# Dense and dilated attention on one core: closer local tiles, contiguous raised copies and three more blocks a period on VectorE

## The chip, the core and the metric

The kernel runs on one core of a Trainium2 chip. The metric is the device time of one execution in microseconds (us), the median of several runs. The kernel before has a median of 811.33 us over 3 runs (809.96 to 811.34). A core has a matrix engine (TensorE, PE in the profile), a vector engine (VectorE, DVE), an engine for exponentials and the like (ScalarE, ACT), a general one (GpSimd, POOL) and one that issues transfers (SyncE, SP).

## What is computed

Two attentions over the same input of 2048 positions and 512 columns, both with 32 heads of 16 columns, are mixed by a gate for each position. The first ("A") attends to all positions. The second ("B", the local one) attends to 8 positions, two apart, up to the own one. All tensors are bfloat16.

```python
def reference(A_x, A_wqkv, A_wo, B_x, B_wqkv, B_wo, gate_w):
    ...
        scores = jnp.einsum("bhqd,bhkd->bhqk", q, k) * (Dh ** -0.5)
        p = _softmax(scores, axis=-1)
        o = jnp.einsum("bhqk,bhkd->bhqd", p, v)
    ...
        W, dil = 8, 2
    ...
        logits = jnp.einsum("bhsd,bhswd->bhsw", q, kg) * scale
        logits = jnp.where(mask[None, None, :, :], logits, -1e9)
        attn = _softmax(logits, axis=-1)
        o = jnp.einsum("bhsw,bhswd->bhsd", attn, vg)
    ...
    g = _sigmoid((x * gate_w).sum(-1, keepdims=True))
    return g * a + (1 - g) * b
```

## The kernel before

**Dense attention.** The work is cut into 32 *periods*: 4 chunks of 512 queries by 8 groups of 4 heads. A period has 64 *blocks*, one for each of 16 key tiles (128 keys) and 4 heads. A block is a score matmul (128 keys by 512 queries, into PSUM), an exponential, and a matmul with the values into the period's accumulator. Blocks reach ACT in *sets*, by turns of 3 and 2 (`set_sizes`), in two PSUM areas (`ring`); one ACT instruction takes a set and writes `pT` in bfloat16.

**Blocks on VectorE.** Some blocks of each period are not given to ACT. `n_dve` says how many: from 3 in the first periods to 12 in all from the seventh on. These are always blocks of the last key tiles (`dve_tiles`, 4 tiles by 4 heads, so 16 at most), in groups of 3 (`NGR`). `d_set` makes them. The score matmul writes a PSUM bank. A *first pass* (`p1`) on DVE scales the scores and writes them as 16-bit integers whose bits, read as bfloat16, approximate the exponential; they go to a buffer of 3 x 512, `dt_a` or a part of `wkv` (whose weights are no longer needed by then). When a group of 3 is full, three *raises* (`sh`, m = 1 to 3) add a constant 32 m to the integers and write the sum into one of three buffers in `pd_a`. PE multiplies the group and each raised copy by values weighted for that copy (`vd_all`), four products for each block, and their sum mends most of the approximation's error. A buffer of `pd_a` has 3 rows of 514 elements (`ROW`), of which 512 are used; the raise reads its input as 6 runs of 256 and writes 3 runs of 512 with a gap of 2 between rows.

At the end of a period DVE transposes the accumulator (`accT`), POOL (DVE in the last two periods) scales it into `ott`, and every second period DVE transposes that into `oat`.

**Local attention.** `b_tile(t)` makes 16 tiles of 128 positions. PE projects keys, values and queries, DVE evicts them (`kvs`, `kvs`, `qb`), SyncE stores keys and values to DRAM and loads them back shifted for the window, in halves (`ksh`, `vsh`; three buffers). POOL does products and sums (`prod`), subtracts the maximum (`lg<-lg,mx`), ACT takes the exponential (`lg<-lg`), DVE sums (`ssum`, `rr`), POOL normalises, weighs the values and adds (`av`, part of it by accumulating transfers that POOL issues), ending in `obb`; PE transposes that and DVE copies it to `obt`. When a chunk's dense and local parts are there, PE multiplies both by the output weights, DVE evicts, SyncE stores.

**What sets the order.** Every piece of work is an `Op` with engine, estimated cost (`occ` or `parts`), due time and dependencies. `list_schedule` plans all engines against each other: an operation that can start, with the earliest due time, goes next. The code is emitted in the planned order, and each engine keeps it: an engine that waits for an instruction holds up all that stand behind it. A pair `(True, x)` in `parts` is planned on a port that DVE and POOL are taken to share, `(False, x)` is not. Due times of the dense part come from `S0`, a running count of blocks on ACT. Those of local tile t come from `BT[t]`, which begins at `b_start` and grows by `b_space`; the release is 70 us ahead of it. PE also gets matmuls of zeros (`z`) in gaps, planned so that it stays active.

Nearly all instructions are issued through two helpers: line 367 for DVE, ACT, POOL and SyncE, line 376 for matmuls (line 1200 and 633 for transposes on PE). So the profile's groups are told apart by tile names.

Of the kernel before, what the change touches and what calls it, by code (L numbers as in the profile page):

```python
# [16 lines left out]

CFG = dict(
    set_sizes=(3, 2),
    n_dve=(3, 3, 6, 6, 9, 9, 12, 12) + (12,) * 24,  # L20
    dve_tiles=4,
    b_start=36.0,
    b_space=(44.0,) * 4 + (47.0,) * 4 + (49.0,) * 8,
    chain=("pe", "dve", "act", "pool", "sp"),
)

# [4 lines left out]
DIL = 2  # L31
QW = 512
NEG = -1.0e9
BITS = 128.0
LN2 = 0.6931471805599453
SHIFT = 175.0
# [2 lines left out]
NGR = 3  # L39
# [3 lines left out]
ROW = QW + 2  # L43
# [3 lines left out]
NPD = 3  # L47
# [7 lines left out]
def _ap(base, dims):  # L55
    return bass.AP(tensor=base.tensor, offset=base.offset, ap=[list(d) for d in dims])
# [51 lines left out]
PVU, PVN = 100.0, 4  # L108
GP = lambda kind, n: [(False, PRE), (True, NS[kind] * n)]
SB = lambda n: [(True, 0.065 + n / 3840.0)]  # L110
TT = lambda n: [(True, 0.075 + n / 960.0)]
PASS, SWITCH, KEEP, RIDE, ALONE = 0.22, 0.1, 1.2, 50.0, 3.0
WAIT, FREE, LATE, CLAMP = 0.15, 0.1, 10.0, -1.0
# [3 lines left out]
SH_LAT = 0.3  # L117
# [187 lines left out]
def kernel(  # L305
# [69 lines left out]
    def mm(out, lhsT, rhs, start, stop, **kw):  # L375
        return chain(nc.tensor.matmul(out, lhsT=lhsT, rhs=rhs, start=start, stop=stop, **kw))  # L376
# [16 lines left out]
    def op(eng, occ, fn, dl, **kw):  # L393
        if any(tk.kind == "misc" for tk in kw.get("use", ())):
            dl -= URG[eng]
        o = Op(eng, occ, fn, dl, **kw)
        ops.append(o)
        return o
# [17 lines left out]
    n_dve = cfg["n_dve"]  # L416
# [3 lines left out]
    for pi in range(NP):  # L420
        first_unit.append(nu)
        n = n_dve[pi]
# [14 lines left out]
    for pi, (own, groups) in enumerate(seq):  # L437
        n = sum(len(g) for g in groups)
# [54 lines left out]
    pd_a = const.tile([128, (NPD + NPG) * NGR * ROW], BF16, name="pd_a")  # L493
# [181 lines left out]
    def k_bound(i, dl):  # L675
# [15 lines left out]
        def fill(s0, s1):  # L691
            def s():
                V.tensor_scalar(out=kt_all[:, i, s0:s1], in0=kt_all[:, i, s0:s1], scalar1=rowc[:, 1:2],
                                scalar2=negk[:, i:i + 1], op0=ALU.mult, op1=ALU.add)
            return s
# [3 lines left out]
        if i == 0:  # L699
            o_k[i] = [op("dve", 0.0, fill(sc * QW, (sc + 1) * QW), dl + 0.1 * sc, deps=[c], parts=SB(QW)) for sc in range(NC)]  # L700
        else:
            o_k[i] = [op("dve", 0.0, fill(0, S), dl, deps=[c], parts=SB(S))] * NC

    o_k = {}

    def k_pair(i, dl, rel):
# [48 lines left out]
        for e in range(2):  # L755
            o_k[i + e] = [op("dve", 0.0, fill(e), dl + 3.0 + 20.0 * e, deps=[m], parts=SB(S))] * NC

# [14 lines left out]
    def v_proj(h0, h1, tb, TB, tag, dl, rel=0.0):  # L772
# [34 lines left out]
        if nt > 0:  # L807
            d = op("dve", 0.0, evd, dl + 2.0, deps=[c], parts=TT((NV - 1) * nt * (h1 - h0) * (DH + 1)))
            for t in range(t0, tb + TB):
# [14 lines left out]
    def q_proj(pi, tag, dl, rel=0.0):  # L824
# [24 lines left out]
        c = op("dve", 0.61, ev, dl - 0.5, deps=[b], use=[tk, tq])  # L849
        o_q[pi] = op("dve", 0.0, ab, dl, deps=[c], use=[tq], parts=SB(QW))  # L850

# [3 lines left out]
    def q_pair(pi, dl, rel):  # L855
# [42 lines left out]
        c = op("dve", 0.61, ev, dl - 7.0, deps=[a], alloc=[tqs], use=[tk])  # L898
        b = op("dve", 0.0, ab, dl - 6.8, deps=[c], alloc=[tqa], use=[tqs], parts=SB(QW))
        np_ = 0.5 if i < NK1 else 1.0  # L900
# [54 lines left out]
    def b_tile(t):  # L955
# [75 lines left out]
        def logits_out(hf, wp):  # L1031
            def s():
# [5 lines left out]
                if hf == 1 and wp + WP == WH and t * 128 < DIL * (W - 1):  # L1038
                    G.affine_select(out=lg[:], in_=lg[:], compare_op=ALU.is_ge, fill=NEG,
                                    base=t * 128, pattern=[[0, H], [-DIL, W]], channel_multiplier=1)  # L1040
# [115 lines left out]
        for g_ in range(len(halves)):  # L1156
# [5 lines left out]
        a = op("dve", 0.34, sm_pre, tb + SMD, deps=[l1], use=[tlg])  # L1162
        a = op("dve", 0.0, sm_sub, tb + SMD, deps=[a], use=[tlg], parts=TT(H * W)) if SM_V else op(
            "pool", 0.0, sm_sub, GFIRST, deps=[a], use=[tlg], parts=GP("ff", H * W))
# [4 lines left out]
        if SM_V:  # L1169
            a = op("dve", 0.1, sm_gate, tb + SMD, deps=[a, o_g])  # L1170
            a = op("dve", 0.0, sm_mul, tb + SMD, deps=[a], use=[tlg], parts=TT(H * W))
        else:
# [117 lines left out]
    d_st, d_last, d_sh = {}, [None, None], []  # L1290
    d_count, d_ends, d_sg = [0, 0, 0, 0], [], []

    def d_set(pi, gi, t, j, qk_, tn):

        c_, i = periods[pi]
        late = pi >= LATE0
        key = (pi, gi)
        first = key not in d_st
        if first:
            slot = d_count[0] % NDL if late else d_count[2] % NDE  # L1300
            d_count[0] += late
            d_count[2] += not late
            d_st[key] = dict(dt=dt_bufs[slot], td=tok("dtl", NDL) if late else tok("dt", NDE), js=[], ts=[], p1=[])
        g = d_st[key]
        n_ = len(g["js"])
        g["js"].append(j)
        g["ts"].append(t)

        st = {}
        tx = tok("misc", 2)  # L1310

        def dq():
            st["x"] = misc_ps([128, QW])
            mm(st["x"][:], kt_all[32 * j:32 * j + 32, i, t * 128:(t + 1) * 128], qt_tiles[pi][32 * j:32 * j + 32, :],
               True, True, tile_position=(32 * j, 0))

        def p1():
            V.tensor_scalar(out=g["dt"][:, n_ * QW:(n_ + 1) * QW].bitcast(U16), in0=st["x"][:], scalar1=float(DH) ** -0.5 * BITS / LN2,
                            scalar2=(127.0 + DEXP + SHIFT * float(DH) ** -0.5 / LN2) * BITS, op0=ALU.mult, op1=ALU.add)
        deps = [o_q[pi], o_k[i][t // TPC], o_vd[(4 * i + j, t)]]  # L1320
        if first and late and d_count[0] <= NDL:
            deps += wkv_users + d_ends[-NV * NDE:]
        a = op("pe", 0.0, dq, tn - 3.0, mode="r", js=[j], deps=deps, alloc=[tx] + ([g["td"]] if first else []),
               use=[q_tok[pi]] + ([] if first else [g["td"]]), after=[qk_, d_last[1]], ride=True, name=f"dq{pi}")
        d_last[1] = a
        o = op("dve", 0.61, p1, tn + P1D, deps=[a], use=[tx, g["td"]], after=[d_last[0]], name=f"p1_{pi}")
        d_last[0] = o
        g["p1"].append(o)
        if len(g["js"]) < NGR:
            return  # L1330
        vs = [o_vd[(4 * i + j_, t_)] for t_, j_ in zip(g["ts"], g["js"])]

        def on_pool(m):
            return m == NV - 1 and gi in POOL_G

        def sh(m, pb):
            def s():
                o_, i_ = pb.bitcast(U16)[:, :, 0:QW], g["dt"].bitcast(U16)
                i_ = _ap(i_, [list(i_.ap[0]), [QW // 2, 2 * NGR], [1, QW // 2]])
                (G if on_pool(m) else V).tensor_scalar(out=o_, in0=i_, scalar1=STEP * m, scalar2=None, op0=ALU.add)  # L1340
            return s

        def pv(m, pb):
            def s():
                for n1, (t_, j_) in enumerate(zip(g["ts"], g["js"])):
                    pv_mm(pi, t_, j_, pb[:, n1, 0:QW], vd_all[:, m - 1, t_ - (NT - NTD)] if m else vp_all[:, t_])
            return s

        def dpv(m, pb, deps, use, dl):
            b = op("pe", 0.0, pv(m, pb), dl, mode="c", js=g["js"], full=1, deps=deps + [o_t0[pi]] + vs,  # L1350
                   use=[use, acc_tok[pi]], name=f"dpv{pi}")
            o_pv[pi].append(b)
            d_ends.append(b)
        dpv(0, g["dt"].rearrange("p (q n) -> p q n", q=NGR), list(g["p1"]), g["td"], tn + 4.5)
        for m in range(1, NV):
            if on_pool(m):
                pb = pd_bufs[NPD + d_count[3] % NPG]
                d_count[3] += 1
                tp = tok("pg", NPG)
                a = op("pool", 0.0, sh(m, pb), GFIRST, deps=list(g["p1"]), alloc=[tp], use=[g["td"]], name=f"sg{pi}",  # L1360
                       after=d_sg[-1:], parts=GP("one", NGR * QW))
                d_sg.append(a)
            else:
                pb = pd_bufs[d_count[1] % NPD]
                d_count[1] += 1
                tp = tok("pd", NPD)
                a = op("dve", 0.0, sh(m, pb), tn + 1.5 + SHD * (m - 1), deps=list(g["p1"]), alloc=[tp], use=[g["td"]],
                       lat=0.065 + NGR * QW / 1920.0 + SH_LAT, after=d_sh[-1:],
                       parts=[(False, 0.065 + NGR * QW / 1920.0)], name=f"sh{pi}")
                d_sh.append(a)  # L1370
            dpv(m, pb, [a], tp, tn + 4.5 + SHD * m)

    pend, dwait = [], []
    for k, us in enumerate(sets):
        ring = "rA" if k % 2 == 0 else "rB"
        n = len(us)
# [34 lines left out]
    for pi, (c_, i) in enumerate(periods):  # L1411
# [37 lines left out]
        if by_v:  # L1449
            a = op("dve", 0.0, po2a, E + 4.0, deps=[a, o_gr], use=[tr_], parts=TT(BPC))  # L1450
            a = op("dve", 0.0, po2b, E + 4.0, deps=[a], alloc=al, use=us, parts=TT(BPC * DH))
        else:
# [139 lines left out]
```

## Time and profile before

| | |
|---|---|
| median of 3 runs | 811.33 us |
| the profiled execution | 811.55 us |
| its span, first to last instruction | 809.7 us |
| granted TensorE clock, mean | 0.995 |
| blocks on ACT (340 sets of 3, 340 of 2) | 1700 |
| blocks on DVE (`p1`), raises | 348, 348 |
| start of the last local tile's exponential on ACT | 743.98 us |

A page of the profile gives busy time and share of the span for each engine, then the chain of work that ended last, followed back from the last instruction. The groups have one line for each kind of instruction: line, engine, operation, output <- inputs (partitions x elements and type), count, then busy time in all and mean in ns of one, then the engine's idle time before them and what ended it. Timelines have the start, the time from the first start to the last end of equal instructions that follow each other, the instruction, its count, and in brackets the idle time before it with what released it. Busy shares in the table of windows are us in that stretch, followed by the granted clock of PE, the share of the transfer engines, and GB/s. An instruction's duration holds a little overlap with the next of its engine, so the distance between starts is what a further one costs.

### The profile page before, as it was taken

The numbers are of one execution on the slowest core, as the hardware profiler recorded it, in microseconds if no ns is written. First come the engines' busy times: TensorE is split into PE (matmuls) and PEld (weight loads), VectorE is DVE, ScalarE is ACT, GpSimd is POOL, SyncE is SP. The second block draws the span as 40 slices with busy tenths as digits, with TensorE's granted clock in tenths as the row PEclk, the third lists the DMA queues.
The fourth block names the chain that finished last, engine by engine and source line by source line (L and its number), as shares of the span: only waits on it lengthen the run. The fifth ranks groups of instructions, "written<-read, shape, count | busy, mean of one in ns | idle before, by whom it ended". The sixth has DMA issues, their size and how long they took to land.

```text
span 809.7 us, 17412 instructions
## 1 busy us (share of the span) xinstructions
PE 744.5 (92%) x6637; PEld 241.5 (30%) x6694; DVE 695.4 (86%) x1080; ACT 782.8 (97%) x704; POOL 633.0 (78%) x1067
## 2 busy tenths in 40 slices
PE   8999999999989999989999999998988999889897
PEld 4333333332322222222222222222222222222232
DVE  5638786989886999999988899898998999898896
ACT  3999999999999999999999999999999999999996
POOL 4097979999979699599999469899989419899910
PEclk9999999999999999999999999999999999999999
DMA  7503071635244432526352433616271422522000
GB/s 262 138 13 111 25 173 42 147 101 143 81 96 106 92 96 73 147 85 138 98 121 62 93 99 111 136 53 139 66 176 33 105 90 67 132 60 73 1 1 27
DMA packets 58883, 77.17 MB, mean 95 GB/s; under 512 B 3744, under 2 KB 50848, under 8 KB 58800
## 3 DMA queue, kind: packets, MB, share of 16 engines
q1 hardware_dynamic: 52608, 53.91, 21.4%
q0 software_dynamic: 6048, 22.02, 14.4%
q8 instruction: 52, 0.85, 0.4%
q14 instruction: 31, 0.25, 0.1%
q10 hardware_dynamic: 144, 0.13, 0.0%
HBM read 43.78 MB, written 10.26 MB: 67 GB/s over the span
## 4 chain that ended last, share of the span: by engine, by line
ACT 49%; PE 27%; issue 20%; DVE 2%; DMA 1%; SPq 0%; ACTq 0%
ACT pT L367 49%; PE misc_ps L376 18%; PE ring L376 8%; DMA xld<-in_A_x_dram 1%; DVE pd_a L367 1%; ACT lg L367 1%; DVE accT L367 0%; PE pxt L633 0%; DVE kt_all L367 0%; DVE wkv L367 0%; DVE dt_a L367 0%; ACT xT L367 0%; SPq L367 0%; DVE qa L367 0%; DVE oat L367 0%
## 5 line engine op out<-in xcount | busy, mean ns | idle before, releaser
L367 ACT ACTIVATE pT<-ring 128x1536 bf16<-128x1536 f32 (+1 forms) x680 | 775.0, 1331 | 10.9 <-PE ring L376 7.3
L376 PE MATMUL ring<-qt,kt_all 32*128 32x512 bf16 x1700 | 268.7, 383 | 48.0 <-ACT pT L367 40.4
L367 POOL TENSOR_TENSOR prod<-ksh,qb 128x256 f32<-128x256 bf16 x256 | 171.5, 726 | 46.0 <-DMA ksh<-kv_scr 35.5
L376 PE MATMUL misc_ps<-pT,vp_all 128*17 128x512 bf16 (+1 forms) x1700 | 207.0, 385 | 0.1
L376 PEld LDWEIGHTS <-kt_all 32*128 32x128 bf16 x2048 | 90.6, 91 | 301.9 <-issue 294.0
L367 DVE TENSOR_SCALAR pd_a<-wkv 128x1536 uint16<-128x1536 uint16 x192 | 175.4, 941 | 0.6
L367 POOL TENSOR_TENSOR prod<-prod 128x256 f32<-128x256 f32 (+1 forms) x256 | 169.7, 679 | 5.2
L367 DVE TENSOR_SCALAR wkv<-misc_ps 128x512 uint16<-128x512 f32 x192 | 129.2, 682 | 24.2 <-PE misc_ps L376 21.8
L367 DVE TENSOR_SCALAR pd_a<-dt_a 128x1536 uint16<-128x1536 uint16 x156 | 142.6, 941 | 3.5 <-PE misc_ps L376 2.7
L376 PE MATMUL misc_ps<-z 128*32 128x512 bf16 x412 | 136.7, 390 | 1.6 <-DVE z L367 1.6
L376 PE MATMUL misc_ps<-pd_a,vd_all 128*17 128x512 bf16 x1044 | 135.1, 382 | 0.6 <-DVE pd_a L367 0.5
L376 PE MATMUL misc_ps<-qt,kt_all 32*128 32x512 bf16 x348 | 128.7, 382 | 4.3 <-DVE accT L367 2.1
L367 DVE TENSOR_SCALAR dt_a<-misc_ps 128x512 uint16<-128x512 f32 x156 | 104.5, 683 | 23.8 <-PE misc_ps L376 21.7
L367 POOL TENSOR_TENSOR prod<-vsh,lg 128x256 f32<-128x256 bf16 x128 | 82.2, 746 | 0.0
L376 PEld LDWEIGHTS <-vp_all 128*17 128x17 bf16 (+1 forms) x2048 | 53.5, 88 | 83.3 <-issue 71.6
L367 POOL TENSOR_TENSOR av<-vsh,lg 128x256 f32<-128x256 bf16 x128 | 77.6, 642 | 0.0
L376 PE MATMUL misc_ps<-bw,xT 128*128 128x512 bf16 x160 | 50.1, 384 | 1.7 <-issue 1.1
L376 PEld LDWEIGHTS <-vd_all 128*17 128x17 bf16 x1044 | 35.4, 88 | 54.3 <-issue 45.7
L376 PEld LDWEIGHTS <-z 128*32 128x32 bf16 x412 | 36.2, 96 | 46.5 <-issue 24.6
L376 PEld LDWEIGHTS <-xT 128*128 128x128 bf16 x576 | 29.1, 97 | 33.3 <-issue 29.5
L376 PE MATMUL misc_ps<-wkv,vp_all 128*17 128x512 bf16 x192 | 31.5, 384 | 0.0
L367 DVE CAST kvs<-misc_ps 128x512 bf16<-128x512 f32 x32 | 21.9, 684 | 10.8 <-PE misc_ps L376 10.8
(97 smaller groups left out, 519.6 us busy)
## 6 DMA issues: line engine op xcount, KB each, us to landing
ksh<-kv_scr SPq DMA_DIRECT2D x32, 512.0 KB
vsh<-kv_scr SPq DMA_DIRECT2D x32, 512.0 KB
av<-prod POOLq DMA_DIRECT2D x28, 512.0 KB, 5.6
av<-av POOLq DMA_DIRECT2D x14, 512.0 KB, 4.6
kv_scr<-kvs SPq DMA_DIRECT2D x16, 256.0 KB
qt<-q_scr SPq DMA_DIRECT2D x30, 128.0 KB
out_dram<-osb SPq DMA_DIRECT2D x15, 128.0 KB
xld<-in_A_x_dram SPq DMA_DIRECT2D x3, 512.0 KB
```

What stands on the lines that cost most here:

```text
L367: return chain_on(key, f(*a, **k))
L376: return chain(nc.tensor.matmul(out, lhsT=lhsT, rhs=rhs, start=start, stop=stop, **kw))
```

## The change

Three things are changed. The distances of local tiles become 43 us for all 16, where they were 44 (four), 47 (four) and 49 (eight). The last three periods (29, 30 and 31, from `FLAT0` on) give 15 blocks instead of 12 to DVE. In these three periods a raise reads 1536 elements in one run and writes 1536 in one run, without the gap between rows, into the same buffers; the planner costs it at 0.1 + 1536 / 3840 us on the shared port, where the others have 0.065 + 1536 / 1920 us off it.

```diff
-    n_dve=(3, 3, 6, 6, 9, 9, 12, 12) + (12,) * 24,
+    n_dve=(3, 3, 6, 6, 9, 9, 12, 12) + (12,) * 21 + (15,) * 3,
...
-    b_space=(44.0,) * 4 + (47.0,) * 4 + (49.0,) * 8,
+    b_space=(43.0,) * 16,
...
+FLAT0 = 29
...
+PT = lambda n: [(True, 0.1 + n / 3840.0)]
...
                 o_, i_ = pb.bitcast(U16)[:, :, 0:QW], g["dt"].bitcast(U16)
-                i_ = _ap(i_, [list(i_.ap[0]), [QW // 2, 2 * NGR], [1, QW // 2]])
+                if pi < FLAT0:
+                    i_ = _ap(i_, [list(i_.ap[0]), [QW // 2, 2 * NGR], [1, QW // 2]])
+                else:
+                    o_ = o_.rearrange("p q n -> p (q n)")
...
                 pb = pd_bufs[d_count[1] % NPD]
+                if pi >= FLAT0:
+                    k0 = d_count[1] % NPD * NGR * ROW
+                    pb = pd_a[:, k0:k0 + NGR * QW].rearrange("p (q n) -> p q n", q=NGR)
...
-                       lat=0.065 + NGR * QW / 1920.0 + SH_LAT, after=d_sh[-1:],
-                       parts=[(False, 0.065 + NGR * QW / 1920.0)], name=f"sh{pi}")
+                       lat=(0.065 + NGR * QW / 1920.0 if pi < FLAT0 else 0.1 + NGR * QW / 3840.0) + SH_LAT, after=d_sh[-1:],
+                       parts=[(False, 0.065 + NGR * QW / 1920.0)] if pi < FLAT0 else PT(NGR * QW), name=f"sh{pi}")
```

## The prediction

> **What bounds the kernel now.** I read the page first: its head, the busy shares and the chain that ended last.
>
> ```profile
> span 809.7 us, 17412 instructions
> PE 744.5 (92%) x6637; PEld 241.5 (30%) x6694; DVE 695.4 (86%) x1080; ACT 782.8 (97%) x704; POOL 633.0 (78%) x1067
> ...
> ACT 49%; PE 27%; issue 20%; DVE 2%; DMA 1%; SPq 0%; ACTq 0%
> ```
>
> ScalarE (ACT) is busy for 97% of the span. Only an engine that makes ACT wait can cost time, and only work taken from ACT can win any. So the next views are what ACT does, grouped by shape, and what it waits for.
>
> ```profile
> L367 ACT ACTIVATE pT<-ring 128x1536 bf16<-128x1536 f32 x340 | 524.0, 1541 | 9.8 <-PE ring L376 6.3 <-PE misc_ps L376 2.9
> L367 ACT ACTIVATE pT<-ring 128x1024 bf16<-128x1024 f32 x340 | 380.8, 1120 | 1.2 <-PE ring L376 1.0
> ...
> ACT pT L367 <- PE ring L376: 7.3, 9, 4.4
> ACT osb L367 <- PE misc_ps L376: 3.8, 1, 3.8
> ACT pT L367 <- PE misc_ps L376: 2.9, 3, 1.5
> ```
>
> The 680 exponentials hold 340 x 3 + 340 x 2 = 1700 blocks of 512 columns. Of the 7.3 us, 4.4 us is the one wait ahead of the first exponential; so between first and last they stall for 7.3 - 4.4 + 2.9 = 5.8 us in all. Their price is read from ACT's timeline, where instructions overlap a little and the distance of starts counts.
>
> ```profile
> 743.98 0.49 ACT L367 ACTIVATE lg<-lg 128x256 f32<-128x256 f32 x1
> 744.28 27.30 ACT L367 ACTIVATE pT<-ring 128x1536 bf16<-128x1536 f32 x24
> 771.81 29.79 ACT L367 ACTIVATE pT<-ring 128x1536 bf16<-128x1536 f32 x26 [0.23 <-PE ring L376]
> 805.41 1.07 ACT L367 CAST osb<-misc_ps 128x512 bf16<-128x512 f32 x2 [3.81 <-PE misc_ps L376]
> ```
>
> Twenty-four sets, by turns of 3 and 2, are 60 blocks in 27.30 us: **0.455 us a block**, gapless. The last one ends at 771.81 + 29.79 = 801.60; from there to 809.7 runs a tail of 8.1 us. Around the span lie 811.55 - 809.7 = 1.85 us in this execution (811.55 against a median of 811.33).
>
> **Part one: nine blocks leave ACT.** Three periods give 15 instead of 12 blocks to VectorE (DVE): ACT has 9 fewer exponentials, 9 x 0.455 = **4.1 us**. The built program agrees: 1691 blocks in 677 sets. On PE a moved block has a score and four products (one per weighted copy) where it had a score and one: 9 x 3 = 27 matmuls more, beside 412 on zeros that fill time which PE has to spare, so no cost there. The gain is real only if DVE keeps up in these periods. PE's filling, and DVE near the end:
>
> ```profile
> L376 PE MATMUL misc_ps<-z 128*32 128x512 bf16 x412 | 136.7, 390 | 1.6 <-DVE z L367 1.6
> ...
> 778.91 0.70 DVE L367 STREAM_TRANSPOSE accT<-misc_ps 128x512 f32<-128x512 f32 x1
> 785.60 1.28 DVE L367 TENSOR_SCALAR wkv<-misc_ps 128x512 uint16<-128x512 f32 x2
> 793.02 5.24 DVE L367 TENSOR_SCALAR pd_a<-wkv 128x1536 uint16<-128x1536 uint16 x6
> 802.08 0.72 DVE L367 STREAM_TRANSPOSE accT<-misc_ps 128x512 f32<-128x512 f32 x1 [3.82 <-PE misc_ps L376]
> ```
>
> A first pass out of PSUM costs 1.28 - 0.68 = 0.60 us of pitch, a raise (5.24 - 0.94) / 5 = 0.86 us. Twelve of each are 17.5 us, in a period of 52 x 0.455 = 23.7 us; the last raise ends 3.8 us ahead of the last transpose.
>
> **Part two: raises written contiguously.** No row shows such a raise. The nearest rows are these:
>
> ```profile
> L367 DVE TENSOR_SCALAR pd_a<-wkv x192: 892/943/955, 243.2 to 797.3; 128x1536 uint16<-128x1536 uint16 x192
> L367 DVE TENSOR_SCALAR kt_all<-kt_all,rowc,negk x11: 406/812/1219, 17.6 to 177.7; 128x2048 bf16<-128x2048 bf16 x7, 128x512 bf16<-128x512 bf16 x4
> L367 DVE TENSOR_SCALAR qa<-qs x15: 278/586/2496, 22.8 to 727.5; 128x256 uint32<-128x256 uint32 x15
> 37.11 0.81 DVE L367 TENSOR_SCALAR kt_all<-kt_all,rowc,negk 128x2048 bf16<-128x2048 bf16 x1
> ```
>
> The second is contiguous in and out: 0.81 us for 2048 columns against 0.41 for 512, 0.26 ns a column. Scaled to 1536 that is 0.41 + 1024 x 0.26 = 0.68 us, with two pointer scalars that a raise lacks. The other bound: if today's 0.94 us is a fixed 0.14 and a rate that doubles, 0.14 + 0.40 = 0.54 us. I take **0.57**, nearer the lower end (both scalars of a raise are constants), so a pitch of 0.49. At the far ends stand 0.94 (nothing gained) and 0.54. Then 15 x 0.60 + 15 x 0.49 = 16.4 us in a period of 49 x 0.455 = 22.3 us: DVE is freer than before, and its saving is off the path. The cover is this slack of some 4 us after the transposes and gate work (1.5 us); without the faster raise it would be 15 x (0.60 + 0.86) + 1.5 = 23.4 us, more than the period.
>
> The rows also say what speaks against this form. Today's raise takes 892 to 955 ns whether GpSimd (POOL) works or, as at 793, does not. The masking of qa, contiguous too, takes 278 ns at best, 586 at the median and 2496 at worst. [...]
>
> **Part three: local tiles follow closer.** Nothing is added: 16 tiles, planned 43 us apart instead of 44, 47 and 49. Where they stand now, and POOL's gaps:
>
> ```profile
> 364.70 0.63 POOL L367 TENSOR_TENSOR lg<-lg,mx 128x256 f32<-128x256 f32 x1
> 404.10 0.63 POOL L367 TENSOR_TENSOR lg<-lg,mx 128x256 f32<-128x256 f32 x1
> 412.82 0.50 ACT L367 ACTIVATE lg<-lg 128x256 f32<-128x256 f32 x1
> 443.88 0.63 POOL L367 TENSOR_TENSOR lg<-lg,mx 128x256 f32<-128x256 f32 x1 [0.18 <-DVE mx L367]
> 452.63 0.52 ACT L367 ACTIVATE lg<-lg 128x256 f32<-128x256 f32 x1
> 473.13 2.56 POOL L367 TENSOR_TENSOR prod<-ksh,qb 128x256 f32<-128x256 bf16 x4 [9.13 <-DVE qs L367]
> 662.94 0.22 POOL L367 TENSOR_TENSOR rden<-rden,g_rw 128x16 f32<-128x16 f32 x1 [15.02 <-DVE rden L367]
> 770.39 1.43 POOL L367 TENSOR_TENSOR obb<-av 128x256 bf16<-128x256 f32 x2
> ```
>
> Where tiles already follow closely POOL turns one out in 39.4 to 39.8 us; elsewhere it idles, 9 and 15 us at a time. In the built order of ACT, the local softmax's exponentials stood after block 120, 198 ... 1488, 1575; now after 120, 193 ... 1363, 1455: 90 blocks a tile between second and last, 90 x 0.455 + 0.3 = 41.3 us. POOL fits with 1.5 us to spare, and its result is ready 8.1 us before ACT asks (404.10 + 0.63 to 412.82). So I charge ACT **nothing**; cover is this 8 us lead, and gone it would cost ACT whatever POOL overruns. The last tile's exponential moves 120 blocks, 54.6 us, forward to 689; POOL's last sum, which ends 27.8 us after it now (771.8 - 744.0), ends at about 717. Period 29 starts at block 1544, about 730: contiguous raises meet POOL only in the scaling of attention outputs of two periods. SyncE's queue gets the same transfers, ksh and vsh nearer to each other and moved past q_scr and out_dram stores; a late qt is what could hurt, and has the lead of two periods.
>
> DVE's work on a tile is packed closer too. Its rows, and those for what this can do:
>
> ```profile
> L367 DVE CAST kvs<-misc_ps 128x512 bf16<-128x512 f32 x32 | 21.9, 684 | 10.8 <-PE misc_ps L376 10.8
> L367 DVE COPY obt<-misc_ps 128x512 bf16<-128x512 bf16 x16 | 6.6, 410 | 0.0
> ...
> 300.00:350.00 50.00, 46.76 (x404) 13.72 (x407) 49.28 (x74) 50.00 (x46) 39.33 (x68) 1.00 0.36 93
> 235.00:245.00 10.00, 9.74 (x70) 2.52 (x73) 7.92 (x14) 8.78 (x9) 7.65 (x14) 0.87 0.69 167
> 565.00:575.00 10.00, 9.77 (x73) 2.81 (x72) 8.60 (x14) 8.77 (x8) 9.69 (x18) 0.83 0.10 28
> 233.92 0.37 PE L376 MATMUL misc_ps<-qt,kt_all 32*128 32x512 bf16 x1 [1.88 <-DVE accT L367]
> 234.25 0.61 PE L376 MATMUL misc_ps<-z 128*32 128x512 bf16 x1
> ```
>
> Three evictions of 0.68 and four short operations of about 0.4 us each (copy, two reductions, a reciprocal) are 3.6 us a tile, in 41.3 instead of some 47 us: 0.25 us more in a period of 23.7 us until 717, then none. At 300 to 350 DVE is busy for 49.3 of 50 us and ACT never waits. But twice, at a period's turn, PE stood still (1.88 us for a transpose on DVE), its granted clock fell to 0.87 and 0.83 in those stretches, matmuls took 0.61 us, and ACT lost 10 - 8.78 = 1.2 us in each. These are accidents of the order, and the order is new from block 120 on. I take their number as unchanged, bounds from none (5.8 us of stalls gone) to four more (4 x 1.2 = 4.9 us).
>
> **The sum.** 811.55 - 4.1 - 0 - 0 = 807.4; against the median 811.33, 807.2. I say **807.3 us**.
>
> **Rivals.**
> First, *more stalls at turns of periods* (slower): DVE is denser until 717, a transpose or raise comes late, PE stands still behind it in order (with the next scores queued behind), the clock falls. For: the row at 233.92. Against: 300 to 350 above. From 3.4 more such accidents on (4.1 / 1.2) the gain is gone; with six more, 807.3 + 7.2 = 814.5. The place is between 200 and 717.
> Second, *POOL falls behind* (slower): at over 41.3 us a tile the lead of 8 us melts, over 14 tiles from 41.9 us each on (8 / 14); at 42.5 ACT waits 14 x 1.2 - 8 = 9 us, 816. For: waits of POOL on its own accumulating transfers. Against: 39.4 us when close.
> Third, *the contiguous raise is no faster*, by its form or by a busy POOL: 23.4 us of DVE against 22.3 of ACT, 1.1 us a period, 3.3 in all; 810.6, no change.
> Fourth, *stalls vanish too*, because DVE and PE are relieved in the last 90 us and the turns fall otherwise: up to 3 us of the 5.8; 804.3.
>
> **How the numbers follow.** Forecast 0.64 (its own range 805.6 to 809.0), fourth 0.13, third 0.08, first 0.11, second 0.04. A difference under 0.2%, 1.6 us, can't be told from none here. Faster than 809.7: the forecast, the fourth, and a little of the third, 0.78; same 0.10, from the third and a mild first; slower 0.12. The range takes in the fourth at 804.3 and the third at 810.6 and leaves out the two slower ones, 0.15, and some 0.05 below: 804.0 to 810.8.
>
> **What would show it.** ACT: 677 exponentials, busy about 4 us less, stalls between first and last of 4 to 8 us. Raises of 128x1536 in two groups, the 45 contiguous ones near 0.57 us and none over 1.5; last raise some 5 us ahead of the last transpose. POOL's last sum near 717, POOL at nought after about 760. POOL's lead before each ACT lg still 6 us or more. Wrong would be: ACT waits named "POOL lg", clock below 0.9 in more than two stretches of 10 us, or raises near 0.94 us.

## The result and the profile after

| | before | after |
|---|---|---|
| median | 811.33 us | **805.6 us** (4 runs, 805.02 to 807.22) |
| ratio | 1 | 0.9937, 95% interval 0.9919 to 0.9955 |
| the profiled execution | 811.55 us | 805.02 us |
| its span | 809.7 us | 803.2 us |
| blocks on ACT, on DVE | 1700, 348 | 1691, 357 |

The changed kernel is faster by 0.63%; the forecast was 807.3, its range 804.0 to 810.8. Two executions among the runs below took several times as long as the rest (3393 us in `e1_space`, whose only profile is of it and is not read here, and 2054 us in `e4_flat12`); the ratios leave them out. In the listing after, the helper's line is 369 and that of matmuls 378. First the head of the page of the changed kernel.

```profile
span 803.2 us, 17445 instructions
...
PE 742.8 (92%) x6651; PEld 240.5 (30%) x6708; DVE 689.1 (86%) x1098; ACT 778.0 (97%) x701; POOL 634.5 (79%) x1067
```

ACT still bounds the kernel at 97%, with 4.8 us less work than before (782.8). The next three views are the groups of exponentials by shape, what ACT waited for (total us, times, longest), and ACT's timeline from the last local tile on.

```profile
L369 ACT ACTIVATE pT<-ring 128x1536 bf16<-128x1536 f32 x338 | 518.8, 1535 | 8.1 <-PE ring L378 5.2 <-PE misc_ps L378 2.2
L369 ACT ACTIVATE pT<-ring 128x1024 bf16<-128x1024 f32 x338 | 376.8, 1115 | 0.8 <-PE misc_ps L378 0.5
L369 ACT ACTIVATE pT<-ring 128x512 bf16<-128x512 f32 x1 | 0.7, 679 | 0.0
```

```profile
ACT pT L369 <- PE ring L378: 5.2, 4, 4.4
ACT osb L369 <- PE misc_ps L378: 3.9, 1, 3.9
ACT pT L369 <- PE misc_ps L378: 2.7, 4, 1.5
```

```profile
685.77 0.50 ACT L369 ACTIVATE lg<-lg 128x256 f32<-128x256 f32 x1
...
708.17 1.02 ACT L369 ACTIVATE pT<-ring 128x1024 bf16<-128x1024 f32 x1 [0.21 <-PE misc_ps L378]
709.95 84.57 ACT L369 ACTIVATE pT<-ring 128x1536 bf16<-128x1536 f32 x75 [0.75 <-PE misc_ps L378]
798.42 1.07 ACT L369 CAST osb<-misc_ps 128x512 bf16<-128x512 f32 x2 [3.90 <-PE misc_ps L378]
```

There are 677 exponentials with 338 x 5 + 1 = 1691 blocks. The last 75 sets hold 37 x 3 + 37 x 2 + 1 = 186 blocks in 84.57 us: 0.455 us a block again, and without a gap from 710 to 794.5, all through the three periods with 15 blocks on DVE. Stalls between first and last exponential are 5.2 - 4.4 + 2.7 = 3.5 us, where they were 5.8. So the span's 6.5 us are 4.1 us of blocks and 2.3 us of stalls. The rest is small: the first exponential's wait is the same 4.4, and the tail from the last exponential (794.52) to the end is 8.7 against 8.1, so 0.6 us longer.

DVE and POOL in the same stretch follow. The first view gives the raises of the last three periods (min, median and max in ns), the second and third are timelines of DVE and POOL.

```profile
L369 DVE TENSOR_SCALAR pd_a<-wkv x30: 495/552/562, 736.1 to 793.2; 128x1536 uint16<-128x1536 uint16 x30
L369 DVE TENSOR_SCALAR pd_a<-dt_a x15: 548/551/749, 731.5 to 788.9; 128x1536 uint16<-128x1536 uint16 x15
```

```profile
789.94 1.49 DVE L369 TENSOR_SCALAR pd_a<-wkv 128x1536 uint16<-128x1536 uint16 x3
...
792.68 1.03 DVE L369 TENSOR_SCALAR pd_a<-wkv 128x1536 uint16<-128x1536 uint16 x2 [0.30 <-PE misc_ps L378]
795.09 0.72 DVE L369 STREAM_TRANSPOSE accT<-misc_ps 128x512 f32<-128x512 f32 x1 [1.37 <-PE misc_ps L378]
```

```profile
676.75 0.63 POOL L369 TENSOR_TENSOR lg<-lg,mx 128x256 f32<-128x256 f32 x1 [0.46 <-DVE mx L369]
...
711.74 1.42 POOL L369 TENSOR_TENSOR obb<-av 128x256 bf16<-128x256 f32 x2
...
753.17 0.41 POOL L369 TENSOR_TENSOR rden<-rden,g_rw 128x16 f32<-128x16 f32 x1 [21.32 <-DVE rden L369]
```

A contiguous raise takes 0.55 us, with a pitch of (1.49 - 0.55) / 2 = 0.47. POOL's last sum ends at 713.2, before the first of the 45 contiguous raises (731.5); its result for the last local softmax was ready 685.77 - 677.38 = 8.4 us before ACT used it. Last, the windows of 10 and 20 us: busy time and instructions of PE, its loader, DVE, ACT and POOL, then the granted TensorE clock and the DMA share.

```profile
235.00:245.00 10.00, 9.56 (x79) 2.76 (x76) 8.70 (x15) 10.00 (x11) 8.90 (x16) 1.00 0.66 120
565.00:575.00 10.00, 9.84 (x85) 2.46 (x84) 9.73 (x16) 10.00 (x10) 9.68 (x16) 1.00 0.55 108
700.00:710.00 10.00, 8.41 (x72) 2.22 (x70) 7.06 (x12) 9.04 (x9) 9.26 (x16) 0.83 0.00 1
740.00:760.00 20.00, 18.43 (x179) 5.56 (x173) 16.19 (x29) 20.00 (x19) 1.03 (x2) 1.00 0.01 2
```

The two stretches of lowered clock before the change are at full clock now, with ACT at 10.00 of 10. A new one has come at a turn of periods (700 to 710; ACT 9.04). The stalls agree. By ACT's timelines the two accidents before cost 0.58 + 0.50 + 0.45 + 0.27 = 1.8 us at 234 to 239 and 1.02 + 0.20 = 1.2 us at 568 to 571; the one after costs 0.21 + 0.75 = 1.0. That is 2.0 of the 2.3 us.

### The profile page after: what moved, and what is told of

Read it like the earlier page. It is cut to its first block, busy times and chain, and to the rows that moved or that the text cites. A ratio compares the mean times of both kernels' runs of the same rounds, so it can differ in the third digit from the quotient of the medians.

```text
span 803.2 us, 17445 instructions
## 1 busy us (share of the span) xinstructions
PE 742.8 (92%) x6651; PEld 240.5 (30%) x6708; DVE 689.1 (86%) x1098; ACT 778.0 (97%) x701; POOL 634.5 (79%) x1067
## 4 chain that ended last, share of the span: by engine, by line
ACT 50%; PE 25%; issue 22%; DVE 2%; DMA 1%; SPq 0%; ACTq 0%
ACT pT L369 49%; PE misc_ps L378 17%; PE ring L378 8%; DMA xld<-in_A_x_dram 1%; ACT lg L369 1%; DVE pd_a L369 0%; DVE wkv L369 0%; DVE kt_all L369 0%; PE pxt L635 0%; DVE dt_a L369 0%; DVE vd_all L369 0%; DVE vp_all L369 0%; ACT xT L369 0%; SPq L369 0%; DVE ssum L369 0%
## 5 line engine op out<-in xcount | busy, mean ns | idle before, releaser
L378 PE MATMUL misc_ps<-pT,vp_all 128*17 128x512 bf16 (+1 forms) x1691 | 201.6, 384 | 0.3 <-DVE dt_a L369 0.2
L369 POOL TENSOR_TENSOR prod<-ksh,qb 128x256 f32<-128x256 bf16 x256 | 174.4, 752 | 27.4 <-DMA ksh<-kv_scr 24.5
L369 POOL TENSOR_TENSOR prod<-prod 128x256 f32<-128x256 f32 (+1 forms) x256 | 172.0, 687 | 5.9
L369 DVE TENSOR_SCALAR pd_a<-wkv 128x1536 uint16<-128x1536 uint16 x198 | 169.1, 882 | 2.2 <-PE misc_ps L378 1.7
L369 DVE TENSOR_SCALAR wkv<-misc_ps 128x512 uint16<-128x512 f32 x198 | 132.3, 682 | 27.2 <-PE misc_ps L378 25.6
L369 DVE TENSOR_SCALAR pd_a<-dt_a 128x1536 uint16<-128x1536 uint16 x159 | 140.3, 905 | 0.9
L378 PE MATMUL misc_ps<-z 128*32 128x512 bf16 x399 | 132.3, 388 | 1.6 <-DVE z L369 1.6
L378 PEld LDWEIGHTS <-z 128*32 128x32 bf16 x399 | 34.9, 96 | 44.8 <-issue 23.4
L369 POOL TENSOR_TENSOR rden<-rden,g_rw 128x16 f32<-128x16 f32 x30 | 8.8, 292 | 41.8 <-DVE rden L369 41.7
L378 PE MATMUL misc_ps<-wkv,vp_all 128*17 128x512 bf16 x198 | 33.8, 384 | 0.0
```

The costliest lines, as they stand in the source:

```text
L369: return chain_on(key, f(*a, **k))
```

## The experiments

Two theories stood against each other at first. **A**: the nine blocks bring 4.1 us, and they need the faster raise only so that DVE keeps up at the end; closer tiles keep POOL out of the way of the contiguous raises, and the rest of the gain is stalls that the new order happens not to have. **B**: closer tiles themselves bring much of the gain. Each text below names its own theories, so a letter can stand for something else in the next one. All diffs are against the changed kernel. The medians of the kernel before, run beside each group, were 811.62 us (first four), 811.03 (next four) and 811.25 (last four).

### Closer tiles alone, and with contiguous raises

`e1_space` has the spacing of 43 us and nothing else of the change:

```diff
-    n_dve=(3, 3, 6, 6, 9, 9, 12, 12) + (12,) * 21 + (15,) * 3,
+    n_dve=(3, 3, 6, 6, 9, 9, 12, 12) + (12,) * 24,
-FLAT0 = 29
+FLAT0 = 99
```

> The changed kernel without the 15 blocks and without contiguous raises: only the spacing of 43 us is left. Theory A (4.1 us of the gain are the nine blocks taken from ACT, the other 1.6 us are stalls at period turns that the new order happens not to have): 809.7 us, 1700 blocks on ACT, one stretch with a granted clock below 0.9 instead of two. Rival B (local work out of the last 90 us is itself what pays): 807.5 or less. Rival C (closer tiles cost, and the rest hides it): 812 or more.

Measured: 809.39 us, ratio 0.9973 (0.9961 to 0.9985). `e4_flat12` has the first two of these four lines alone: 12 blocks everywhere, the last three periods contiguous, 43 us.

> The changed kernel with 12 instead of 15 blocks in the last three periods, contiguous raises and 43 us kept. Theory A: nine blocks back on ACT, 805.6 + 4.1 = 809.7, equal to the kernel with the spacing alone; DVE idle for some 6 us more in each of the three periods. Rival F (a freer DVE at the end speeds PE and ACT by itself): 807.5 or less.

Measured: 809.49 us, 0.9975 (0.9964 to 0.9985), the same as without contiguous raises. A window of its trace says why:

```profile
740.00:760.00 20.00, 17.98 (x159) 5.83 (x156) 11.80 (x21) 19.98 (x19) 0.84 (x2) 1.00 0.01 2
```

DVE is idle for 8.2 of 20 us there, and ACT waits 3.8 us for its last input, as before. A faster raise is worth nothing by itself: nothing on the path waits for it. Closer tiles alone are worth some 2 us (811.62 - 809.39 = 2.2), near the 1.6 of theory A and well short of the 3.8 or more of theory B. From `e4_flat12` to the changed kernel, which differ in the nine blocks alone, lie 809.49 - 805.6 = 3.9 us (3.7 from the median 809.33 without its long execution), against 9 x 0.455 = 4.1 as forecast.

### The other two parts with the old spacing

`e2_oldspace`:

```diff
-    b_space=(43.0,) * 16,
+    b_space=(44.0,) * 4 + (47.0,) * 4 + (49.0,) * 8,
```

> The changed kernel with the old spacing of 44, 47 and 49 us: 15 contiguous raises a period run while POOL still works until about 770 us. Theory A (DVE has some 4 us of slack a period, so waiting for POOL is absorbed): 811.3 - 4.1 = 807.2, at most 808.5; contiguous raises in the first two of the three periods between 0.55 and over 1 us. Rival D (without a silent POOL the contiguous raise is worth nothing, DVE becomes the bound): 810.5 or more. Rival B (spacing itself pays): also above 809.

Measured: 811.46 us, 1.0003 (0.9994 to 1.0013): the whole gain is gone, and theory A's 807.2 to 808.5 with it. B and D both allowed this time. The raises of its last three periods, POOL's last sum, and ACT's last wait:

```profile
L369 DVE TENSOR_SCALAR pd_a<-wkv x30: 544/583/1082, 737.4 to 798.2; 128x1536 uint16<-128x1536 uint16 x30
L369 DVE TENSOR_SCALAR pd_a<-dt_a x15: 543/752/1085, 732.8 to 793.2; 128x1536 uint16<-128x1536 uint16 x15
```

```profile
778.49 2.05 POOL L369 TENSOR_TENSOR obb<-av 128x256 bf16<-128x256 f32 x2
```

```profile
ACT osb L369 <- PE misc_ps L378: 7.1, 1, 7.1
```

Here POOL works until 780.5, in two of the three periods. Raises beside it take up to 1.08 us instead of 0.55, and the same sum of POOL 2.05 us instead of 1.42. What is late lands in the wait ahead of the last output, 7.1 us instead of 3.9, as theory D has it. These 3.2 us are the larger part of the 5.2 by which the two profiled executions differ in span (808.4 and 803.2); another 1.2 are stalls between exponentials (4.7 and 3.5), and the rest was not traced. So spacing is worth 811.46 - 805.6 = 5.9 us when the other parts are there, and some 2 when they are not.

### Fifteen blocks with the old raise

`e3_gapped15`:

```diff
-FLAT0 = 29
+FLAT0 = 99
```

> The changed kernel with the raises of the last periods written with gaps as before, still 15 blocks there. Theory A (15 x 1.46 + 1.5 = 23.4 us of DVE against 22.3 of ACT): 1.1 us a period lost, 805.6 + 3.3 = 808.9, DVE without idle time from about 730 on. Rival E (DVE's real slack is larger, the contiguous form is not needed): 805.6 to 806.4.

Measured: 812.91 us, 1.0023 (1.0011 to 1.0035). That is slower than before, by more than theory A's 808.9 allowed for. ACT's last wait, and DVE's timeline at two places:

```profile
ACT osb L369 <- PE misc_ps L378: 11.1, 1, 11.1
```

```profile
734.25 0.71 DVE L369 STREAM_TRANSPOSE accT<-misc_ps 128x512 f32<-128x512 f32 x1
...
801.82 5.24 DVE L369 TENSOR_SCALAR pd_a<-wkv 128x1536 uint16<-128x1536 uint16 x6
807.55 0.72 DVE L369 STREAM_TRANSPOSE accT<-misc_ps 128x512 f32<-128x512 f32 x1 [0.49 <-PE misc_ps L378]
```

From the transpose of period 28 to that of period 31 DVE needs 807.55 - 734.25 = 73.3 us, 24.4 a period, where ACT needs 49 x 0.455 = 22.3. ACT isn't held up in between. It runs ahead, and the backlog of three periods, some 6 to 7 us, is paid at the very end: the last wait is 11.1 - 3.9 = 7.2 us longer than in the changed kernel, as the medians are apart (812.91 - 805.6 = 7.3). The profiled execution is the slowest of twelve, 816.91 us. Its other 4 us lie ahead of 730, as 3.8 us more of stalls, where the traces of both kernels have the same instructions in the same order on DVE, ACT and POOL; so they belong to that execution and not to the raises.

`e9_lastflat` tests that reading. Only the last period is contiguous:

```diff
-FLAT0 = 29
+FLAT0 = 31
```

> As the changed kernel, but of the three periods with 15 blocks only the last one writes its raises contiguously. Theory A (a gapped raise costs nothing where it stands; its price is a backlog on VectorE of some 2 us a period, paid only when no slack follows): periods 29 and 30 leave about 4 us of backlog, and the last period, with contiguous raises, has some 4 us of slack (16.4 + 1.5 of 22.3 us) and works it off. 805.6 to 807.5, and the wait ahead of the last output falls from 11.1 us (all gapped) to under 6. Rival D (each gapped period costs its third of the 7.3 us between the two kernels wherever it stands): 805.6 + 4.9 = 810.5, with the time lost in waits of ScalarE in periods 29 and 30.

Measured: 808.48 us, 0.9965 (0.9951 to 0.9979), between the two theories. DVE's last two transposes of accumulators:

```profile
783.79 0.71 DVE L369 STREAM_TRANSPOSE accT<-misc_ps 128x512 f32<-128x512 f32 x1
...
800.75 0.72 DVE L369 STREAM_TRANSPOSE accT<-misc_ps 128x512 f32<-128x512 f32 x1 [1.45 <-PE misc_ps L378]
```

The last period takes DVE 800.75 - 783.79 = 17.0 us instead of 22.3, so a later period does work off a backlog. Not all of it: ACT's last wait is 7.1 us against the "under 6" that was expected, 3.2 over the changed kernel's 3.9, and the medians are 2.9 apart. (The profiled execution took 810.11; it has 1.6 us more of stalls ahead of 730, again in the same order of instructions.) No stall of ACT shows in the two gapped periods beyond 0.23 us, so rival D's way of paying is not what happens. Between the transposes of periods 28 and 31 DVE takes 65.8 us in the changed kernel, 69.2 here, 70.2 in `e2_oldspace` and 73.3 in `e3_gapped15`; the last waits are 3.9, 7.1, 7.1 and 11.1. The longer DVE needs for the three periods, the longer the last wait.

### Contiguous raises beside a busy POOL

`e5_flat8` writes raises contiguously from period 8 on:

```diff
-FLAT0 = 29
+FLAT0 = 8
```

> The changed kernel with contiguous raises in all periods from the ninth on (FLAT0 = 8), so 300 of them while POOL works. Theory A (a contiguous raise and a POOL instruction hold each other up): raises beside a busy POOL spread from 0.55 to over 1 us with a median above 0.7, POOL's busy time up from 634.5 by more than 30 us because its instructions are stretched, local tiles later (the planned order already puts the last local exponential after block 1618 instead of 1455), 809 us or more. Rival G (no such hold-up on the chip): raises at 0.55 us throughout, POOL's busy time unchanged, 805.5 us or less.

Measured: 847.43 us, 1.0462 (1.0441 to 1.0482). Its busy shares, its raises, and ACT's waits:

```profile
PE 760.0 (90%) x6671; PEld 240.2 (28%) x6728; DVE 704.7 (83%) x1098; ACT 781.5 (92%) x701; POOL 709.5 (84%) x1067
```

```profile
L369 DVE TENSOR_SCALAR pd_a<-wkv x198: 495/882/4453, 243.7 to 834.3; 128x1536 uint16<-128x1536 uint16 x198
L369 DVE TENSOR_SCALAR pd_a<-dt_a x159: 496/943/3769, 33.9 to 831.1; 128x1536 uint16<-128x1536 uint16 x159
```

```profile
ACT pT L369 <- PE ring L378: 20.9, 16, 4.4
ACT pT L369 <- PE misc_ps L378: 16.9, 18, 4.3
ACT osb L369 <- PE misc_ps L378: 12.4, 1, 12.4
```

Each engine stretches the other: raises up to 4.45 us, POOL's 1067 instructions 709.5 us instead of 634.5. The median raise, 0.88 and 0.94 us, is hardly better than a gapped one at 0.94. Theory A's hold-up is shown, and raises suffer far more than in `e2_oldspace`, where none took over 1.09. The longest raise, and POOL beside it:

```profile
539.29 4.45 DVE L369 TENSOR_SCALAR pd_a<-wkv 128x1536 uint16<-128x1536 uint16 x1
539.13 2.84 POOL L369 TENSOR_TENSOR prod<-ksh,qb 128x256 f32<-128x256 bf16 x4
541.65 1.67 POOL L369 TENSOR_TENSOR prod<-prod 128x256 f32<-128x256 f32 x2
```

It stands there while six instructions of POOL follow each other. How much of the 42 us is this hold-up and how much the planner's other order, which puts the local tiles later, this run does not separate.

### Going further in the same direction

`e6_four` gives 15 blocks and contiguous raises to the last four periods, `e12_five` to the last five:

```diff
-    n_dve=(3, 3, 6, 6, 9, 9, 12, 12) + (12,) * 21 + (15,) * 3,
+    n_dve=(3, 3, 6, 6, 9, 9, 12, 12) + (12,) * 20 + (15,) * 4,
-FLAT0 = 29
+FLAT0 = 28
```

```diff
-    n_dve=(3, 3, 6, 6, 9, 9, 12, 12) + (12,) * 21 + (15,) * 3,
+    n_dve=(3, 3, 6, 6, 9, 9, 12, 12) + (12,) * 19 + (15,) * 5,
-FLAT0 = 29
+FLAT0 = 27
```

> The changed kernel with 15 blocks and contiguous raises in the last four periods instead of three. Theory A: three more blocks off ACT, 3 x 0.455 = 1.4 us, POOL beside DVE only until about 713 in a period that begins at 706: 804.2. Rival D (any contiguous raise beside POOL costs what it saves): 805.6 or more.

> As the changed kernel, but 15 blocks and contiguous raises in the last five periods. The fifth period runs from about 686 to 709, where GpSimd works nearly without a gap. Theory A (a contiguous raise is held up by GpSimd's instructions, 0.8 to 1.1 us each as in the run with the old spacing): VectorE needs 15 x (0.60 + 0.9) + 1.5 + 2 = 26 us there of 22.3, a backlog of 4 us that the next period takes up; so neither gain nor loss against four periods by more than 1.4 us: 802.4 to 804.5, raises up to 1.1 us. Rival C (both engines stretch each other, as where all periods from the eighth on were contiguous: raises up to 4 us, GpSimd's last tile late): 806 or more.

Measured: 803.81 us, 0.992 (0.9906 to 0.9933), for four periods, and **802.53 us**, 0.9895 (0.9879 to 0.9912), for five. Both are faster than the changed kernel by their medians, the second beyond its interval (0.9919 to 0.9955); the intervals of four and five just overlap. The fifth period from the end meets a busy POOL. Its raises, and POOL's last sum, in `e12_five`:

```profile
L369 DVE TENSOR_SCALAR pd_a<-wkv x12: 544/992/1084, 684.2 to 706.4; 128x1536 uint16<-128x1536 uint16 x12
L369 DVE TENSOR_SCALAR pd_a<-dt_a x4: 544/894/974, 694.8 to 707.8; 128x1536 uint16<-128x1536 uint16 x4
```

```profile
721.14 1.41 POOL L369 TENSOR_TENSOR obb<-av 128x256 bf16<-128x256 f32 x2
```

As expected the raises take 0.8 to 1.1 us there, and POOL ends 9.4 us later than in the changed kernel (722.5 against 713.2). Little of it reaches ACT: four contiguous periods with slack follow, and the last wait is 5.2 us, 1.3 over the changed kernel's. A sixth period would have POOL beside its raises for its whole length; that wasn't tried.

### The exact spacing, and the clock

`e7_415` is `e6_four` at 41.5 us; `e10_435` and `e11_425` are the changed kernel at 43.5 and 42.5:

```diff
-    b_space=(43.0,) * 16,
+    b_space=(41.5,) * 16,
```

```diff
-    b_space=(43.0,) * 16,
+    b_space=(43.5,) * 16,
```

```diff
-    b_space=(43.0,) * 16,
+    b_space=(42.5,) * 16,
```

> As the kernel with four periods, with local tiles planned 41.5 us apart instead of 43. Theory A: POOL needs 39.4 us a tile, ends some 11 us earlier (last local exponential after block 1430 instead of 1455) and is silent in all of the last four periods: 804.0 or a little less, POOL's lead before ACT's local exponentials still 6 us or more. Rival (POOL falls behind at this spacing): ACT waits for POOL at lg, lead under 3 us, 807 or more.

> As the changed kernel, local tiles planned 43.5 us apart instead of 43. Theory A (closer tiles matter by where GpSimd's work ends): it ends 15 x 0.5 = 7.5 us later, about 721, still ahead of the contiguous raises; 805 to 806.5, no change. Rival B (what the spacing won is fewer stalls at turns of periods, an accident of the order that is dealt anew): 804 to 809, and whatever differs from 805.6 is found as ScalarE's stalls between first and last exponential.

> As the changed kernel, local tiles planned 42.5 us apart instead of 43. Theory A: GpSimd ends some 7 us earlier, about 706, no change: 805 to 806.5. Rival B (stalls at turns of periods are dealt anew): 804 to 809, and the difference from 805.6 is found as ScalarE's stalls between first and last exponential.

Measured: 806.05 us, 0.9948 (0.9934 to 0.9962) for `e7_415`, slower than `e6_four` though POOL ended some 10 us earlier; none of ACT's waits named POOL, and its stalls between first and last exponential were 6.3 us, one of them 2.9. At 43.5 it is 807.37 us, 0.9944 (0.993 to 0.9958); at 42.5 it is 806.18 us, 0.9946 (0.9926 to 0.9966), in runs from 803.14 to 810.51. These intervals and the changed kernel's overlap, so nothing sets 42.5, 43 and 43.5 apart. The median at 43.5 lies outside theory A's 805 to 806.5 and inside rival B's range; its profiled execution, one of the fastest (805.79), has stalls of 3.6 us and cannot say where the slower ones lost time. What differs from one run to the next of the same program is the granted clock: at 42.5 the two runs with a mean granted clock of 0.999 took 803.1 and 803.2 us, the one at 0.989 took 810.5. The profiled execution had a lowered clock in two windows:

```profile
720.00:730.00 10.00, 8.39 (x81) 2.90 (x77) 8.82 (x15) 10.00 (x10) 0.37 (x2) 0.96 0.14 41
730.00:740.00 10.00, 9.80 (x72) 2.48 (x72) 6.65 (x13) 8.12 (x8) 0.47 (x1) 0.70 0.00 0
```

The traces at 43 us say the same. Until about 705 us the changed kernel, `e3_gapped15`, `e4_flat12`, `e6_four` and `e9_lastflat` have the same instructions in the same order on DVE, ACT and POOL; yet three of these five executions have a stretch of lowered clock at 550 to 560, one has another at 120, and the changed kernel's and `e6_four`'s have neither.

`e8_fill` tries to hold the clock with more matmuls on zeros (542 instead of 399; in the traces the order on DVE is another one from 33 us on):

```diff
-ROWS_SPAN, ROWS_MIN, ROWS_IDLE, ROWS_ADD, ROW_STRIP = 2.3, 6.5, 8.0, 4, 0.25
+ROWS_SPAN, ROWS_MIN, ROWS_IDLE, ROWS_ADD, ROW_STRIP = 2.3, 8.0, 10.0, 6, 0.25
```

> The changed kernel with more matmuls of zeros planned into PE's gaps (542 instead of 399). Theory A (each stretch of lowered clock at a period's turn costs ACT 1.2 us, and more zeros keep the clock up): mean clock 0.999 to 1.0 in nearly all runs, spread of runs below 1 us, 804.4. Rival H (zeros stand in the way of scores): clock up, but stalls of ACT behind PE more numerous, 806 or more.

Measured: 841.61 us, 1.0383 (1.0366 to 1.0399), with ACT's waits

```profile
ACT pT L369 <- PE ring L378: 26.1, 18, 9.2
ACT pT L369 <- PE misc_ps L378: 14.8, 13, 4.4
```

The mean clock fell to 0.985, so neither theory had it: rival H's stalls came, without the higher clock. Whether the lowered clock is cause or effect of these longer waits this run can't say. The planned order is another one too (the last local exponential starts at 746.60 instead of 685.77), so it doesn't single out the matmuls on zeros either. It shows only that planning more of them in this way is not the cure.

## Why the prediction held, point by point

**What bounds the kernel.** Right: what a run gained or lost is found in ACT's blocks and ACT's waits. In `e3_gapped15` and `e9_lastflat` the loss is the wait ahead of the last output, in `e2_oldspace` most of it; in `e5_flat8`, `e7_415` and `e8_fill` most of it is stalls between exponentials.

**Nine blocks leave ACT, 4.1 us.** Right: 0.455 us a block again, and 3.7 to 3.9 us between the two kernels that differ in these blocks alone. PE's 27 added matmuls cost nothing that could be seen.

**Contiguous raises, 0.57 us and a pitch of 0.49.** Right: 0.55 and 0.47. The bound of 0.54, from a fixed 0.14 us and a rate that doubles, and the reason for staying near it, constants as scalars, were the author's estimate; no run takes the 0.55 us apart. That the form's saving lies off the path is shown by `e4_flat12`. The price of being without it, 23.4 us of DVE in a period of 22.3, had the right sign and was mis-sized: measured 24.4. For two such periods of `e3_gapped15`, between transposes, a window and its groups of first passes and raises show this:

```profile
734.20:786.40 52.20, 47.46 (x428) 14.83 (x429) 50.68 (x71) 51.97 (x47) 1.69 (x4) 1.00 0.01 3
```

```profile
L369 DVE TENSOR_SCALAR pd_a<-wkv 128x1536 uint16<-128x1536 uint16 x19 | 17.5, 943 | 0.3 <-PE misc_ps L378 0.3
L369 DVE TENSOR_SCALAR wkv<-misc_ps 128x512 uint16<-128x512 f32 x22 | 15.0, 685 | 0.4
L369 DVE TENSOR_SCALAR pd_a<-dt_a 128x1536 uint16<-128x1536 uint16 x12 | 10.9, 944 | 0.0
L369 DVE TENSOR_SCALAR dt_a<-misc_ps 128x512 uint16<-128x512 f32 x11 | 7.4, 681 | 0.5 <-PE misc_ps L378 0.2
```

DVE was busy for 50.7 of 52.2 us. The 33 first passes and 31 raises, at the forecast's pitches, are 33 x 0.60 + 31 x 0.86 = 46.5 us, so other work is 4.2, about 2 us a period and not 1.5; and 1.5 us in two periods was idle. Over all three periods (busy for 71.0 of 73.3 us, and 45 x 1.46 = 65.7) other work is 1.8 us a period and idle time 0.8: together the 1.0 us that was missed. So three periods cost 7.3 us, not 3.3, and the third rival, had it come true, would have been no tie at 810.6 but the whole gain gone.

**What spoke against the form.** The prediction named the masking of `qa`, which spreads from 278 to 2496 ns. The runs show that contiguous raises and POOL hold each other up: a raise takes 0.55 us beside a silent POOL, 0.89 and 0.99 at the medians beside a busy one in `e12_five`, where two of POOL's sums (`obb<-av`) take 2.10 us beside such raises, instead of 1.42 in the changed kernel. At these medians a raise loses 0.34 and 0.44 us, near the 586 - 278 = 308 ns between the masking's median and its best. How the two share the time is not shown: the raise of 4.45 us in `e5_flat8` stands beside six instructions of POOL.

**Closer tiles, charged at nothing.** As to POOL right: its lead stays at 8 us, no wait of ACT names it. Its last sum came at 713.2 rather than 717, mainly since ACT reached the last tile's exponential 3 us earlier than forecast. What fell short is the step "I take their number as unchanged", said of the stalls at turns: 3.5 us instead of 5.8, less 0.6 us of a longer tail. That was inside its bounds and is most of the fourth rival, which let up to 3 us vanish; it is why the time is 1.7 us under the forecast. That rival's reason, relief in the last 90 us, is not what happened: the accidents that went lay at 234 and 568.

How many accidents one execution has is luck, but not their average. The mean granted clock is 0.9956 over 68 executions with the old spacing (56 of the kernel before, 12 of `e2_oldspace`) and 0.9979 over 46 at 43 us (the changed kernel and the six runs that keep its spacing, `e5_flat8` and `e8_fill` aside). A stretch of 3.4 us at half clock takes 1.7 / 805 = 0.002 off the mean, so by this estimate closer tiles save about one such stretch an execution, at 1.0 to 1.8 us each: most of their 2 us. Why this order has fewer stays open; at 42.5 us the mean is 0.995 again.

**The accidents themselves.** The prediction read both as PE standing still for a transpose on DVE, at 1.2 us. That fits the first, which cost 1.8 us, since its window began after the first loss. Ahead of the second, at 565, PE waited only for ACT, 0.64 and 0.52 us, and so it does ahead of the one after the change:

```profile
705.76 0.39 PE L378 MATMUL ring<-qt,kt_all 32*128 32x512 bf16 x3 [0.96 <-ACT pT L369]
```

There PE was waiting for ACT's exponentials, not the other way round.

**Last raise 5 us ahead of the last transpose.** Wrong: 795.09 - (792.68 + 1.03) = 1.4 us. DVE had become faster than its supply. It waited for PE ahead of the last raise (0.30) and of the transpose (1.37), so the tail is not shorter (8.7 us against 8.1). The step that failed took the margin from DVE's work alone, without when PE brings the last scores.

**The rivals.** More stalls at turns, and POOL falling behind, did not come; the first was met in `e7_415`, which has 6.3 us of such stalls. The third rival named the busy POOL as one of its conditions, so the prediction saw that the raises need closer tiles; it did not see how much hangs on it. It priced spacing at nothing, yet without it (`e2_oldspace`) the change gives nothing.

## What to carry to other kernels

When an engine's work is moved to a second one, look for the backlog in the last wait of the program, not in stalls in the middle: here 2 us a period were invisible until the end and then cost 7. A form of an operation that is faster alone, but that another engine holds up, is worth placing where that engine has ended, here at 0.55 us a raise; beside a busy POOL the gain was gone (811.46 us in `e2_oldspace`) or turned into a loss (847.43 in `e5_flat8`). A part of a change that measures at zero alone, as the contiguous raise does, can still be the condition for the one that pays: test parts by taking one away, not only by adding one.

## What the runs showed of the hardware

**Half clock for 3.4 us, or for twice that.** Three stretches of 3.4 us of the changed kernel, around the turn of periods at 706 (columns as in the windows above):

```profile
702.70:706.10 3.40, 2.01 (x26) 0.64 (x27) 2.84 (x6) 3.40 (x4) 2.73 (x6) 1.00 0.01 2
706.10:709.50 3.40, 3.40 (x26) 0.72 (x23) 2.29 (x3) 2.89 (x3) 3.32 (x6) 0.50 0.00 0
709.50:712.90 3.40, 3.25 (x28) 0.83 (x28) 1.78 (x3) 2.95 (x3) 3.40 (x6) 0.99 0.03 7
```

The clock goes to 0.50 and back after 3.4 us; the 0.83 of a 10 us window is this stretch. The first one before the change, from 234.2 to 237.7 by windows of 0.5 us, has the same length. In `e11_425` the clock stayed at 0.50 for 6.8 us (0.96 and 0.70 in the two windows above). PE had not been idle for the 3.4 us ahead of the stretch at 706: it was busy for 2.01 of them (the page counts 6651 matmuls to 6708 weight loads, so a few records of matmuls may be missing, and it is rather more than less), and its longest pause there was the 0.96 us above. What lowers the clock, and after how long a pause, no run shows.

**The gapped raise is indifferent to POOL.** In `e3_gapped15` all 357 raises took 893 to 956 ns, with POOL busy for 636.6 us beside them. The contiguous one is 0.55 us alone and 0.89 to 0.99 at the median in contact, so beside a busy POOL the gapped form gives up next to nothing, and POOL's busy time stays near the changed kernel's 634.5 us.
